# Batch 0's first tile on its own, the other tiles of its batch a slot or more behind, and two tiles of batch 2 turned by DMA

## The chip, the core and the metric

The kernel runs on one NeuronCore of a Trainium2 chip, as one program. The metric is the device time of one execution in microseconds. The core's engines are named as the profile names them: PE (TensorE, matmuls and transposes), PEld (its weight loads), DVE (VectorE), ACT (ScalarE), POOL (GpSimd) and SP (SyncE, which here only issues DMAs).

## The reference, cut to what matters

```python
# q, k, v: (8 batches, 8 heads, 576 rows, 64); all float32
kv  = einsum('bhsd,bhse->bhde', k, v)              # 64 x 64 for each head
out = einsum('bhsd,bhde->bhse', q, kv)
out = out / sqrt(mean(out*out, -1) + 1e-6) * g_norm
x   = out.transpose(0, 2, 1, 3).reshape(8, 576, 512)
xn  = (x - mean(x)) / sqrt(var(x) + 1e-6) * g_ln   # over the 512
y   = x + relu(xn @ w_ch1) @ w_ch2                 # 512 -> 2048 -> 512
```

A linear attention without a softmax, a normalisation within each head, and a feed-forward block with a layer norm and a residual.

## The kernel before

**Tiles.** A tile is 128 of a batch's rows. Each batch has four full tiles (0 to 3) and a remainder of 64 rows; the remainders of two batches form one tile of a last block called "rem". q, k and v are cast to bf16 by the loads, which POOL issues; matmuls take bf16 and add up in float32 in PSUM.

**From q to x.** For each batch, `kv_of` multiplies k and v and writes the result, two heads to a 128 x 128 block, into `kv_pack`. q is turned (rows to columns) so that it can be the stationary operand: by PE for batches 0 and 1 (`turn_first`, `turn_q`), by one DMA transpose issued by SP for the others (`turn_q_dma`). A tile then goes through the steps of class `Tile`: `o` (four matmuls on PE, into `o_ps`), `sq` (ACT squares it), `red` (DVE sums the squares of each head), `root` (ACT), the reciprocal (DVE, in `inv`), `y`, `x` and `xc` (DVE: divide; times g_norm with the row's sum beside it; minus the mean, times g_ln, in bf16), `var` (ACT, the variance) and `turn`, which brings xc's columns to the partitions as `xT_blk`: by four PE transposes and an ACT copy, or by one DMA transpose issued by SP. The factor 1/sqrt(var) is left out of the first matmul and applied at the very end, in `finish`.

**The two layers.** `mm1` multiplies quarters or less of w1 with xT and ACT writes the Relu into `m1`; `mm2_part` multiplies m1 with w2 into `p2`; `finish` (DVE) scales, adds x, and SP stores the result.

**Order.** The program is recorded as written (no scheduler): each engine runs its own instructions in the order in which the code emits them. `mm1` and `mm2_part` call `tick()`, which counts slots: a slot is one group of matmuls, some 0.9 us of PE work. Before each slot's matmuls `tick()` emits what `at(slot, fn)` has put there: that is how the tiles of later batches are woven into the matmuls of earlier ones. `plan_tile(s, make, turn_at, on_pe)` puts `o`, `sq`, `red` at slot s, `y`, `x`, `xc` at s+2, `var` at s+6, and `turn` at `turn_at`. Batch 0's first layer has slots 0 to 15, its second 16 to 31; batch 1 has 32 to 47 and 48 to 63; batch 2 has 64 to 79 (two tiles at a time) and 80 to 95. From batch 3 on, four tiles go together.

PSUM tiles come from pools that fix how many are in flight: `ps_m` (1), `ps_out` (2), `ps1` (3, `mm1`'s results among them) and `ps2` (2).

**The start.** Batch 0 has its own code. k comes in on SP's and ACT's queues in float32 and is cast by DVE and ACT; POOL issues v in two halves of two head pairs each, then q of rows 0 to 319 (`lo`) in two halves of four heads, w1's first quarter, the rest of q (`up`), the rest of w1, half of w2, batch 1, and the rest of w2. PE runs `fill` matmuls (on zeros, results unused) until data arrive. `kv_first` works by halves of the heads, and so do tiles 0 and 1, side by side: `half_turn` turns both tiles' q, `half_o` multiplies and squares, `half_red` reduces. For these two tiles x comes by a second matmul with kv times g_norm (`kv_g`; `o_g`, `x_g`), so that `y` is not needed. `halves_xc` and `halves_turn` make xT in two halves. The other tiles of batch 0 have their places in the agenda:

```python
at(1, lambda: turn_first(2, ps_m, "misc", nc.vector.tensor_copy))
at(1.1, lambda: halves_turn(1, xc1, ps_out, "ops"))
at(1.2, o2)     # o and sq of tile 2
at(1.3, x2)     # red, y, x, xc of tile 2
at(4, lambda: turn_first(3, ps_m, "misc"))
at(5, lambda: t[3].o())
at(5.1, x3)     # sq, red, y, x, xc of tile 3
at(6, lambda: t[2].turn(True))
at(9, lambda: turn_first(J, ps_m, "misc"))
at(10, lambda: t[3].turn(True))
```

Lines that the prediction names: L126, L127 and L129 load v and q; L196 is a fill; L266 is `sq`, L287 `red`, L297 `root`, L311 `x`, L321 `xc`; L337 and L339 are `turn`'s PE transposes and its ACT copy, L341 its DMA transpose; L402 is `mm1`'s matmul and L405 its Relu; L418 is `mm2_part`'s matmul; L183 is `turn_groups`, L541 `halves_turn`, L260 `o`.

Of the kernel before, what the change touches and what calls it, by code (L numbers as in the profile page):

```python
# [14 lines left out]
def kernel(  # L15
# [70 lines left out]
    def lo(t, b, h0=0, h1=H):  # L86
        return t[b, h0:h1, :S_LO, :].rearrange("h (p j) d -> p h j d", j=JJ)
# [35 lines left out]
    nc.vector.memset(fill_sb, 0.0)  # L123
    nc.sync.dma_start(k_f[:, :HP // 2], pairs(k, 0, HP // 2))
    nc.scalar.dma_start(k_f[:, HP // 2:], pairs(k, HP // 2, HP))
    nc.gpsimd.dma_start(v_p[:, :HP // 2], pairs(v, 0, HP // 2))  # L126
    nc.gpsimd.dma_start(v_p[:, HP // 2:], pairs(v, HP // 2, HP))  # L127
    for h0 in (0, H // 2):
        nc.gpsimd.dma_start(q_in[0][:64, h0:h0 + H // 2], lo(q, 0, h0, h0 + H // 2))  # L129
    load_w1(0)  # L130
    make_identity(nc, identity)
    nc.gpsimd.dma_start(q_in[0][64:, :, :J], up(q, 0))
# [44 lines left out]
    def turn_groups(tp, i, h0, h1):  # L177
        groups = ((0, 2 * i), (0, 2 * i + 1)) if i < 2 else ((64, 2 * i - 4), (64, 2 * i - 3))
        if i == J:
            groups = ((0, J),)  # L180
        for h in range(h0, h1):
            for half, (p0, j) in enumerate(groups):
                nc.tensor.transpose(  # L183
                    tp[h % 2 * D:h % 2 * D + D, (h - h0) // 2, half * 64:half * 64 + 64],
                    q_in[0][p0:p0 + 64, h, j, :], identity[p0:p0 + 64, p0:p0 + 64])
        return 64 * len(groups)
# [3 lines left out]
        n = turn_groups(tp, i, 0, H)  # L190
        copy(qts[0][:, i, :, :n], tp[:, :, :n])  # L191

    def fill(n, pool=ps2, tag="p2"):
        for _ in range(n):
            p1 = pool.tile([128, 512], f32, tag=tag, name="p1")
            nc.tensor.matmul(p1, lhsT=fill_sb[:, :128], rhs=fill_sb, start=True, stop=True)  # L196
            del p1

    def turn_q_dma(b):
        q_p = kv_in.tile([128, JJ, H, D], bf16, tag="qp", bufs=2)  # L200
# [6 lines left out]
    def kv_first():  # L207
        kvp = held[0] = kv_pack[0]
        g = g_norm_sb.to_broadcast([128, HP // 2, D])
        for i, (pe, te, po, to) in enumerate(((ps_m, "misc", ps1, "p1"), (ps1, "p1", ps1, "p1"))):  # L210
            even = pe.tile([128, HP // 2, D], f32, tag=te, name="even")
            odd = po.tile([128, HP // 2, D], f32, tag=to, name="odd")
            hps = slice(i * HP // 2, (i + 1) * HP // 2)
            for hp in range(hps.start, hps.stop):
                for j in range(JP):
                    js = slice(j * D, (j + 1) * D)
                    for hh, dst in ((0, even), (1, odd)):
                        rows = slice(hh * D, hh * D + D)
                        nc.tensor.matmul(dst[rows, hp - hps.start, :], lhsT=k_p[rows, hp, js],
                                         rhs=v_p[rows, hp, js],  # L220
                                         start=(j == 0), stop=(j == JP - 1))
            nc.vector.tensor_copy(kvp[:D, hps, :D], even[:D])
            nc.scalar.copy(kvp[D:, hps, D:], odd[D:])
            nc.vector.tensor_mul(kv_g[:D, hps, :D], even[:D], g[:D])
            nc.vector.tensor_mul(kv_g[D:, hps, D:], odd[D:], g[D:])
            del even, odd

    def kv_of(b):
        kv_ps = ps_m.tile([128, HP, D], f32, tag="misc", name="kv_ps")
# [228 lines left out]
    def at(slot, fn):  # L458
        agenda.setdefault(int(slot), []).append((slot, fn))
# [12 lines left out]
    del gl_row  # L472

    qts[0] = qt_pool.tile([128, JJ, HP, 128], bf16, tag="qt", name="qt")
    fill(18)
    kv_first()


    t = [main_tile(0, i, ps2, "p2") for i in range(4)]
    for i in range(2):  # L480
        t[i].ss = work.tile([128, H, 1], f32, tag="ss", bufs=4, name="ss")
    sqs = [work.tile([128, H, D], f32, tag="sq", name="sq") for _ in range(2)]
    banks = (((ps_out, "ops"), (ps_m, "misc")), ((ps_out, "ops"), (ps1, "p1")))
    copies = ((nc.scalar.copy, nc.scalar.copy), (nc.vector.tensor_copy, nc.vector.tensor_copy))

    def half_turn(half):
        hp0 = half * HP // 2
        tps = [ps2.tile([128, HP // 2, 128], bf16, tag="p2", name="tp") for _ in range(2)]
        for i in range(2):
            turn_groups(tps[i], i, 2 * hp0, 2 * hp0 + H // 2)  # L490
        for i in range(2):
            copies[half][i](qts[0][:, i, hp0:hp0 + HP // 2], tps[i])

    def half_o(i, half):
        hp0 = half * HP // 2
        pool, tag = banks[half][i]
        o = pool.tile([128, H // 2, D], f32, tag=tag, name="o_half")
        flat = o.rearrange("p h e -> p (h e)")
        for k2 in range(HP // 2):
            nc.tensor.matmul(flat[:, k2 * 128:(k2 + 1) * 128], lhsT=qts[0][:, i, hp0 + k2, :],  # L500
                             rhs=kv_pack[0][:, hp0 + k2, :], start=True, stop=True)
        nc.scalar.activation(sqs[i][:, half * H // 2:(half + 1) * H // 2], o, func=AF.Square)

    def half_red(i, half):
        hs = slice(half * H // 2, (half + 1) * H // 2)
        nc.vector.tensor_reduce(t[i].ss[:, hs], sqs[i][:, hs], axis=AX.X, op=ALU.add)

    half_turn(0)
    fill(2, ps_out, "ops")
    half_o(0, 0)  # L510
    half_turn(1)
    half_o(1, 0)
    half_o(0, 1)
    half_red(0, 0)
    half_red(0, 1)
    half_o(1, 1)
    t[0].root()
    half_red(1, 0)
    half_red(1, 1)
    t[0].o_g(ps1, "p1")  # L520
    t[1].o_g(ps1, "p1")
    fill(8)
    t[0].x_g()
    t[1].root()


    def halves_xc(i):
        x_blk, st, _ = t[i].blk
        for c in range(2):
            cs = slice(c * Dm // 2, (c + 1) * Dm // 2)  # L530
            xc = work.tile([128, Dm // 2], bf16, tag="xch", bufs=4, name="xc")
            nc.vector.scalar_tensor_tensor(xc, in0=x_blk[:, i, cs], scalar=st[:, 1, i:i + 1],
                                           in1=g_ln_sb[:, cs], op0=ALU.add, op1=ALU.mult)
            yield xc

    def halves_turn(i, xcs, pool, tag):
        xT = t[i].blk[2]
        for c, xc in enumerate(xcs):
            tp = pool.tile([128, 2, 128], bf16, tag=tag, name="tp")
            for kk in range(2):  # L540
                nc.tensor.transpose(tp[:, kk, :], xc[:, kk * 128:(kk + 1) * 128], identity)  # L541
            nc.scalar.copy(xT[:, 2 * c:2 * c + 2, i * 128:(i + 1) * 128], tp)

    halves_turn(0, halves_xc(0), ps_out, "ops")
    t[1].x_g()
    xc1 = list(halves_xc(1))


    def x2():
        t[2].red()  # L550
        t[2].y()
        t[2].x()
        t[2].xc()

    def x3():
        t[3].sq()
        t[3].red()
        t[3].y()
        t[3].x()
        t[3].xc()  # L560

    def o2():
        t[2].o()
        t[2].sq()
# [119 lines left out]
```

## Time and profile before

| | |
|---|---|
| Time, median of 5 runs | 292.21 us (292.13 to 292.37) |
| The profiled execution's own time | 292.21 us |
| Its span in the profile | 290.4 us |
| Granted TensorE clock | 1.00 |
| PE busy | 281.5 us, 97% of the span |
| ACT, DVE, POOL busy | 155.6, 150.9, 41.1 us |
| Chain that ended last | 84% PE |

Times within the profile count from the span's start. In an order of time, a line gives the start, the duration, the engine, the line of the code, the operation, what it writes and reads, how many such instructions are merged, and in square brackets how long the engine had been idle before and what ended that. A matmul's duration is the time until its result is there; the next one may start earlier, so the starts tell the pace: sixteen matmuls of 128 columns (one slot of the first layer) take 0.893 us from start to start.

### The profile page before, as it was taken

What the parts mean: (1) busy time and instruction counts of PE and PEld (TensorE: products, weight loads), DVE (VectorE), ACT (ScalarE), POOL (GpSimd) and SP (SyncE); (2) the same over time, 40 slices, a digit from 0 to 9 for tenths busy, and PEclk for the clock granted to TensorE, in tenths of its full rate; (3) what the DMA queues carried; (4) which work ended last, traced back from release to release, by engine and by line L of the source; (5) the groups of instructions that cost most, each with busy time, mean ns of one, the idle gap of its engine ahead of it and who ended that gap; (6) DMA issues with size and microseconds to landing.
All of it is one profiled execution on the core that took longest, in us unless ns stands there. A gap on an engine that the chain in (4) does not pass through costs nothing.

```text
span 290.4 us, 5777 instructions
## 1 busy us (share of the span) xinstructions
PE 281.5 (97%) x2294; PEld 159.5 (55%) x2320; DVE 150.9 (52%) x335; ACT 155.6 (54%) x341; POOL 41.1 (14%) x68
## 2 busy tenths in 40 slices
PE   8889999999999999999999999999999999999995
PEld 3579755995578744444444544444444444444444
DVE  5775028936996793666366935752578300220022
ACT  3467755885569931892189408930894066016500
POOL 8522520032050003200410023000000000000000
PEclk9999999999999999999999999999999999999999
DMA  7999999469789818994997279959202510131033
GB/s 213 203 206 205 201 202 219 103 102 191 145 147 193 109 42 150 213 168 88 151 202 107 50 145 198 167 78 168 54 18 53 112 36 0 38 81 27 2 72 72
DMA packets 63290, 35.84 MB, mean 123 GB/s; under 512 B 30748, under 2 KB 58268, under 8 KB 63264
## 3 DMA queue, kind: packets, MB, share of 16 engines
q0 software_dynamic: 28016, 17.76, 44.0%
q1 hardware_dynamic: 34736, 16.99, 30.0%
q10 hardware_dynamic: 512, 0.72, 0.8%
q8 instruction: 18, 0.29, 0.4%
q14 instruction: 8, 0.07, 0.1%
HBM read 36.71 MB, written 9.44 MB: 159 GB/s over the span
## 4 chain that ended last, share of the span: by engine, by line
PE 84%; DVE 5%; DMA 4%; ACT 2%; issue 2%; POOL 0%; SPq 0%; DVEq 0%; POOLq 0%
PE p L402 40%; PE p L418 38%; DMA v_in<-in_v_dram 2%; PE o_ps L260 2%; DMA out_dram<-o_sb 2%; PE kv_ps L235 2%; DVE o_sb L423 1%; DVE ss L287 1%; ACT m L405 1%; DVE x_blk L311 1%; DVE y L292 1%; PE tp L183 1%; DVE xc L321 1%; PE p L196 1%; ACT sq L266 0%
## 5 line engine op out<-in xcount | busy, mean ns | idle before, releaser
L402 PE MATMUL p<-xT_blk,w_sb 128*128 128x128 bf16 (+2 forms) x1017 | 131.7, 285 | 0.9 <-ACT m L405 0.3
L418 PE MATMUL p<-w_sb,m 128*128 128x512 bf16 (+2 forms) x590 | 126.9, 368 | 1.6 <-issue 0.8
L405 ACT ACTIVATE m<-p 128x512 bf16<-128x512 f32 x144 | 85.2, 597 | 41.7 <-PE p L402 39.7
L402 PEld LDWEIGHTS <-w_sb 128*128 128x128 bf16 x1024 | 78.4, 98 | 44.6 <-issue 1.1
L418 PEld LDWEIGHTS <-m 128*128 128x128 bf16 x608 | 56.8, 98 | 61.2
L423 DVE SCALAR_TENSOR_TENSOR o_sb<-p,rstd,x_blk 128x512 f32<-128x512 f32 (+2 forms) x38 | 27.4, 721 | 54.0 <-PE p L418 51.2
L266 ACT ACTIVATE sq<-o_ps 128x512 f32<-128x512 f32 x34 | 20.2, 595 | 41.2 <-PE o_ps L260 41.1
L329 ACT ACTIVATE dev<-x_blk,st_blk 128x512 f32<-128x512 f32 x36 | 25.7, 716 | 4.5 <-DVE st_blk L315 4.4
L287 DVE TENSOR_REDUCE ss<-sq 128x8 f32<-128x512 f32 x34 | 23.1, 679 | 8.4 <-ACT sq L266 8.4
L321 DVE SCALAR_TENSOR_TENSOR xc<-x_blk,st_blk,g_ln_sb 128x512 bf16<-128x512 f32 x34 | 25.6, 752 | 1.2
L292 DVE TENSOR_TENSOR y<-o_ps,inv 128x512 f32<-128x512 f32 x34 | 23.5, 692 | 2.8
L311 DVE SCALAR_TENSOR_TENSOR x_blk<-y,g_norm_sb 128x512 f32<-128x512 f32 x34 | 23.5, 692 | 1.2
L411 DVE RECIPROCAL rstd<-rstd 128x4 f32<-128x4 f32 x9 | 1.6, 175 | 39.3 <-ACT rstd L410 39.3
L304 DVE RECIPROCAL inv<-rms 128x8 f32<-128x8 f32 x36 | 7.2, 201 | 23.1 <-ACT rms L297 23.1
L98 POOL COPY gate<-qt 1x1 bf16<-1x1 bf16 x5 | 0.9, 178 | 114.8 <-DMA qt<-q_p 114.8
L297 ACT ACTIVATE rms<-ss,eps_sb 128x8 f32<-128x8 f32 x36 | 10.7, 298 | 9.8 <-DVE ss L287 9.1
L260 PEld LDWEIGHTS <-qt 128*128 128x128 bf16 (+1 forms) x152 | 10.0, 100 | 7.4 <-issue 1.7
L260 PE MATMUL o_ps<-kv_pack,qt 128*128 128x128 bf16 (+1 forms) x152 | 13.3, 220 | 0.2 <-DVE qt L191 0.2
L196 PE MATMUL p<-fill_sb 128*128 128x512 bf16 x27 | 9.2, 507 | 1.4 <-DVE eps_sb L137 1.2
L339 ACT COPY xT_blk<-tp 128x512 bf16<-128x512 bf16 x10 | 5.8, 580 | 2.3 <-PE tp L337 2.3
L329 ACT ACTIVATION_READ_ACCUMULATOR dev<-x_blk,st_blk 128x1 f32 x36 | 6.9, 191 | 0.0
L196 PEld LDWEIGHTS <-fill_sb 128*128 128x128 bf16 x28 | 3.2, 123 | 6.0 <-issue 3.8
(79 smaller groups left out, 118.3 us busy)
## 6 DMA issues: line engine op xcount, KB each, us to landing
out_dram<-o_sb SPq DMA_DIRECT2D x70, 128.0 KB, 2.4
w_sb<-in_moe_w_ch_dram POOLq DMA_DIRECT2D x8, 512.0 KB, 13.9
k_in<-in_k_dram POOLq DMA_DIRECT2D x7, 320.0 KB, 5.5
v_in<-in_v_dram POOLq DMA_DIRECT2D x7, 320.0 KB, 8.6
q_in<-in_q_dram POOLq DMA_DIRECT2D x7, 320.0 KB, 12.6
q_in<-in_q_dram POOLq DMA_DIRECT2D x8, 256.0 KB, 12.7
k_in<-in_k_dram POOLq DMA_DIRECT2D x7, 256.0 KB, 6.5
v_in<-in_v_dram POOLq DMA_DIRECT2D x7, 256.0 KB, 10.2
```

The source lines that it names most:

```text
L196: nc.tensor.matmul(p1, lhsT=fill_sb[:, :128], rhs=fill_sb, start=True, stop=True)
L260: nc.tensor.matmul(flat[rows, hp * 128:(hp + 1) * 128], lhsT=lhsT_of(hp), rhs=kvp[:, hp, :], start=True, stop=True)
L266: nc.scalar.activation(self.sq_t, self.o_ps, func=AF.Square)
L287: nc.vector.tensor_reduce(self.ss, self.sq_t, axis=AX.X, op=ALU.add)
L292: nc.vector.tensor_mul(self.y_t, self.o_ps, self.inv().to_broadcast([128, H, D]))
L311: nc.vector.scalar_tensor_tensor(x_blk[:, ts].rearrange("p (h d) -> p h d", h=H), in0=self.y_t, scalar=1.0, in1=g_norm_sb.to_broadcast([12 ...
L321: nc.vector.scalar_tensor_tensor(self.xc_t, in0=x_blk[:, self.ts], scalar=st[:, 1, self.ts:self.ts + 1], in1=g_ln_sb, op0=ALU.add, op1=ALU ...
L329: nc.scalar.activation(dev, x_blk[:, ts], func=AF.Square, bias=st[:, 1, ts:ts + 1], accum_out=st[:, 2, ts:ts + 1])
L402: nc.tensor.matmul(p1[:, i, :], lhsT=w1_sb[:, kk, de * 128:(de + 1) * 128], rhs=blk[2][:, kk, sl], start=(kk == 0), stop=(kk == nK - 1))
L405: nc.scalar.activation(m1[:, de0:de0 + per, sl], p1, func=AF.Relu)
L418: nc.tensor.matmul(p2[:, c0:c1], lhsT=m1s[b][:, de, ts * 128:(ts + 1) * 128], rhs=w2_sb[:, de, c0:c1], start=(de == 0), stop=(de == nDe - 1))
L423: nc.vector.scalar_tensor_tensor(o_sb[:, c0:c1], in0=p2[:, c0:c1], scalar=rstds[b][:, ts:ts + 1], in1=blks[b][0][:, ts, c0:c1], op0=ALU.mu ...
```

## The change

- v is loaded as three head pairs, then one; q's rows of tile 0 alone come between the two, and the rest of q's first 320 rows behind them. The number of loads is the same.
- `kv_first` becomes the class `KvFirst`, used for three head pairs and then for one, with its matmuls, copies and products with g_norm as separate steps.
- Tile 0 goes alone through the start. Tile 1's q is turned behind it, its reduction and root stand behind tile 0's xc.
- Slot 1 holds the q turns of tile 2, the remainder and tile 3 (all copied by ACT), tile 2's steps and tile 1's xT; slot 3 holds tile 3's steps (`before_1`, `before_3`).
- The first layer of batch 0 goes in other pieces, with three quarters of tile 2 before the last quarter of tiles 0 and 1; its second layer goes in a half, a quarter and a quarter.
- Fills: 18, 2, 3 and 2, where there were 18, 2 and 8; fills of one call share a PSUM tile.
- Batch 2's tiles start at slots 44, 48, 53 and 58 (before 46, 51, 55 and 59); its tiles 0 and 1 are turned by DMA at slots 50 and 54 instead of by PE at 53 and 58, tiles 2 and 3 by PE at 61 and 67 (before 63 and 68).

```diff
-    nc.gpsimd.dma_start(v_p[:, :HP // 2], pairs(v, 0, HP // 2))
-    nc.gpsimd.dma_start(v_p[:, HP // 2:], pairs(v, HP // 2, HP))
-    for h0 in (0, H // 2):
-        nc.gpsimd.dma_start(q_in[0][:64, h0:h0 + H // 2], lo(q, 0, h0, h0 + H // 2))
+    nc.gpsimd.dma_start(v_p[:, :HP - 1], pairs(v, 0, HP - 1))
+    nc.gpsimd.dma_start(q_in[0][:64, :, :2], lo(q, 0)[:, :, :2])
+    nc.gpsimd.dma_start(v_p[:, HP - 1:], pairs(v, HP - 1, HP))
+    nc.gpsimd.dma_start(q_in[0][:64, :, 2:], lo(q, 0)[:, :, 2:])
...
-    fill(18)
-    kv_first()
-    t = [main_tile(0, i, ps2, "p2") for i in range(4)]
...
+    fill(18)
+    kv_a = KvFirst(0, HP - 1, ((ps_m, "misc"), (ps1, "p1")))
+    kv_b = KvFirst(HP - 1, HP, ((ps1, "p1"), (ps1, "p1")))
+    t = [main_tile(0, 0)] + [main_tile(0, i, *((ps1, "p1") if i == 1 else (ps2, "p2")))
+                             for i in range(1, 4)]
...
+    kv_a.mms()
+    kv_a.copies()
+    turn_first(0, ps2, "p2")
+    kv_a.times_g()
+    fill(2)
+    kv_b.mms()
+    kv_b.copies()
+    part_o(kv_a)
+    part_o(kv_b)
+    part_sq(kv_a)
+    part_sq(kv_b)
+    kv_b.times_g()
+    t[0].o_g(ps2, "p2")
+    part_red(kv_a)
+    part_red(kv_b)
     t[0].root()
-    half_red(1, 0)
-    half_red(1, 1)
-    t[0].o_g(ps1, "p1")
+    turn_first(1, ps_m, "misc")
+    dead = fill(3)
+    t[1].o()
+    t[1].sq()
     t[1].o_g(ps1, "p1")
-    fill(8)
+    fill(2, dead)
+    del dead
     t[0].x_g()
-    t[1].root()
...
     halves_turn(0, halves_xc(0), ps_out, "ops")
+    t[1].red()
+    t[1].root()
     t[1].x_g()
     xc1 = list(halves_xc(1))
...
+    def before_1():
+        turn_first(2, ps_m, "misc")
+        turn_first(J, ps2, "p2")
+        t[2].o()
+        halves_turn(1, xc1, ps_out, "ops")
+        t[2].sq()
+        turn_first(3, ps_m, "misc")
+        x_of(2)
+
+    def x_of(i):
+        t[i].red()
+        t[i].y()
+        t[i].x()
+        t[i].xc()
+
+    def before_3():
+        t[3].o()
+        t[3].sq()
+        x_of(3)
...
-    at(1, lambda: turn_first(2, ps_m, "misc", nc.vector.tensor_copy))
-    at(1.1, lambda: halves_turn(1, xc1, ps_out, "ops"))
-    at(1.2, o2)
-    at(1.3, x2)
-    at(4, lambda: turn_first(3, ps_m, "misc"))
-    at(5, lambda: t[3].o())
-    at(5.1, x3)
+    at(1, before_1)
+    at(3, before_3)
     at(6, lambda: t[2].turn(True))
-    at(9, lambda: turn_first(J, ps_m, "misc"))
...
-    for j, s, tn in ((0, 46, 53), (1, 51, 58), (2, 55, 63), (3, 59, 68)):
-        plan_tile(s, lambda j=j: main_tile(2, j), tn, True)
+    for j, s, tn in ((0, 44, 50), (1, 48, 54), (2, 53, 61), (3, 58, 67)):
+        plan_tile(s, lambda j=j: main_tile(2, j), tn, j > 1)
...
-    for ts, c0, c1 in ((0, 0, 8), (1, 0, 8), (0, 8, 12), (1, 8, 12), (0, 12, 16), (1, 12, 16),
-                       (2, 0, 16), (3, 0, 16)):
+    for ts, c0, c1 in ((0, 0, 4), (1, 0, 4), (0, 4, 8), (1, 4, 8), (0, 8, 12), (1, 8, 12),
+                       (2, 0, 12), (0, 12, 16), (1, 12, 16), (2, 12, 16), (3, 0, 16)):
         mm1(0, ts, 1, c0, c1)
...
-    for ts in range(4):
-        mm2_part(0, ts, p2s[ts], 0, nDe // 2)
+    for de0, de1 in ((0, nDe // 2), (nDe // 2, nDe * 3 // 4)):
+        for ts in range(4):
+            mm2_part(0, ts, p2s[ts], de0, de1)
     for ts in range(4):
         p2 = p2s[ts]
         p2s[ts] = None
-        mm2_part(0, ts, p2, nDe // 2, nDe)
+        mm2_part(0, ts, p2, nDe * 3 // 4, nDe)
         finish(0, ts, p2)
```

`KvFirst` does what `kv_first` did for one half of the heads, with a slice of head pairs of any size; `part_o`, `part_sq` and `part_red` are `half_o` and `half_red` for such a slice of tile 0.

More of the change, by code (lines that the diff above doesn't have):

```diff
@@ L191, in turn_first, with fill @@
         copy(qts[0][:, i, :, :n], tp[:, :, :n])
-    def fill(n, pool=ps2, tag="p2"):
+    def fill(n, p1=None):
+        if p1 is None:
+            p1 = ps2.tile([128, 512], f32, tag="p2", name="p1")
         for _ in range(n):
-            p1 = pool.tile([128, 512], f32, tag=tag, name="p1")
             nc.tensor.matmul(p1, lhsT=fill_sb[:, :128], rhs=fill_sb, start=True, stop=True)
-            del p1
+        return p1
     def turn_q_dma(b):
@@ L205, in turn_q_dma, with __init__, mms, copies @@
         qts[b] = q_t
[L207 to L214, printed above, removed]
+    class KvFirst:
+        def __init__(self, hp0, hp1, pools):
+            self.hps, self.pools = slice(hp0, hp1), pools
+        def mms(self):
+            n = self.hps.stop - self.hps.start
+            (pe, te), (po, to) = self.pools
+            self.even = pe.tile([128, n, D], f32, tag=te, name="even")
+            self.odd = po.tile([128, n, D], f32, tag=to, name="odd")
+            for hp in range(self.hps.start, self.hps.stop):
                 for j in range(JP):
                     js = slice(j * D, (j + 1) * D)
-                    for hh, dst in ((0, even), (1, odd)):
+                    for hh, dst in ((0, self.even), (1, self.odd)):
                         rows = slice(hh * D, hh * D + D)
-                        nc.tensor.matmul(dst[rows, hp - hps.start, :], lhsT=k_p[rows, hp, js],
-                                         rhs=v_p[rows, hp, js],
+                        nc.tensor.matmul(dst[rows, hp - self.hps.start, :],
+                                         lhsT=k_p[rows, hp, js], rhs=v_p[rows, hp, js],
                                          start=(j == 0), stop=(j == JP - 1))
[L222 to L226, printed above, removed]
+        def copies(self):
+            nc.vector.tensor_copy(kv_pack[0][:D, self.hps, :D], self.even[:D])
+            nc.scalar.copy(kv_pack[0][D:, self.hps, D:], self.odd[D:])
+        def times_g(self):
+            g = g_norm_sb.to_broadcast([128, self.hps.stop - self.hps.start, D])
+            nc.vector.tensor_mul(kv_g[:D, self.hps, :D], self.even[:D], g[:D])
+            nc.vector.tensor_mul(kv_g[D:, self.hps, D:], self.odd[D:], g[D:])
+            del self.even, self.odd
     def kv_of(b):
@@ L474 @@
     qts[0] = qt_pool.tile([128, JJ, HP, 128], bf16, tag="qt", name="qt")
+    held[0] = kv_pack[0]
     fill(18)
-    kv_first()
-    t = [main_tile(0, i, ps2, "p2") for i in range(4)]
[L480 to L516, printed above, removed]
+    kv_a = KvFirst(0, HP - 1, ((ps_m, "misc"), (ps1, "p1")))
+    kv_b = KvFirst(HP - 1, HP, ((ps1, "p1"), (ps1, "p1")))
+    t = [main_tile(0, 0)] + [main_tile(0, i, *((ps1, "p1") if i == 1 else (ps2, "p2")))
+                             for i in range(1, 4)]
@@ new lines, with part_o @@
+    t[0].ss = work.tile([128, H, 1], f32, tag="ss", bufs=4, name="ss")
+    sq_0 = work.tile([128, H, D], f32, tag="sq", name="sq")
+    o_0 = {}
+    def part_o(kv_x):
+        hp0, hp1 = kv_x.hps.start, kv_x.hps.stop
+        o_0[hp0] = ps_out.tile([128, 2 * (hp1 - hp0), D], f32, tag="ops", name="o_part")
+        flat = o_0[hp0].rearrange("p h e -> p (h e)")
+        for hp in range(hp0, hp1):
+            nc.tensor.matmul(flat[:, (hp - hp0) * 128:(hp - hp0 + 1) * 128],
+                             lhsT=qts[0][:, 0, hp, :], rhs=kv_pack[0][:, hp, :],
+                             start=True, stop=True)
@@ new lines, in part_sq, with part_red @@
+    def part_sq(kv_x):
+        hp0, hp1 = kv_x.hps.start, kv_x.hps.stop
+        nc.scalar.activation(sq_0[:, 2 * hp0:2 * hp1], o_0.pop(hp0), func=AF.Square)
+    def part_red(kv_x):
+        hs = slice(2 * kv_x.hps.start, 2 * kv_x.hps.stop)
+        nc.vector.tensor_reduce(t[0].ss[:, hs], sq_0[:, hs], axis=AX.X, op=ALU.add)
+    kv_a.mms()
[8 more added lines that the diff above has]
+    part_sq(kv_a)
@@ L544 @@
     halves_turn(0, halves_xc(0), ps_out, "ops")
+    t[1].red()
+    t[1].root()
     t[1].x_g()
     xc1 = list(halves_xc(1))
[L549 to L555, printed above, removed]
-        t[3].sq()
[L557 to L564, printed above, removed]
+    def before_1():
[13 more added lines that the diff above has]
+        t[3].o()
+        t[3].sq()
+        x_of(3)
     def next_loads():
```

## The prediction

> **What bounds the kernel now.** I read the page first, then TensorE's order of time, then ScalarE and VectorE around the place where TensorE fills up, then the late waits and the landings of the first loads.
>
> ```profile
> PE 281.5 (97%) x2294; PEld 159.5 (55%) x2320; DVE 150.9 (52%) x335; ACT 155.6 (54%) x341; POOL 41.1 (14%) x68
> ```
>
> TensorE (PE) is the bound over the span. Its order of time shows from where:
>
> ```profile
> 15.04 0.68 PE L541 MATMUL tp<-identity,xc 128*128 128x128 bf16 x4 [0.84 <-DVE xc L532]
> 15.78 1.34 PE L402 MATMUL p<-xT_blk,w_sb 128*128 128x128 bf16 x16
> 17.05 0.44 PE L183 MATMUL tp<-identity,q_in 64*64 64x64 bf16 x16
> 17.42 0.40 PE L541 MATMUL tp<-identity,xc 128*128 128x128 bf16 x4
> 18.02 0.40 PE L260 MATMUL o_ps<-kv_pack,qt 128*128 128x128 bf16 x4 [0.20 <-DVE qt L191]
> ...
> 33.37 4.48 PE L418 MATMUL p<-w_sb,m 128*128 128x512 bf16 x19
> ```
>
> The first real matmul (slot 0) starts at 15.78, the second layer (slot 16) at 33.37. From 18.02 on PE has only cracks. So the time moves with the start of slot 16, with PE work after it, and with the few waits left. The nearest thing to a wait is on ScalarE, whose queue runs in order (all engines' order of time):
>
> ```profile
> 18.45 0.60 ACT L266 ACTIVATE sq<-o_ps 128x512 f32<-128x512 f32 x1
> 19.09 0.69 DVE L287 TENSOR_REDUCE ss<-sq 128x8 f32<-128x512 f32 x1 [1.12 <-ACT sq L266]
> 19.81 0.30 ACT L297 ACTIVATE rms<-ss,eps_sb 128x8 f32<-128x8 f32 x1 [0.75 <-DVE ss L287]
> ...
> 22.10 0.75 DVE L321 SCALAR_TENSOR_TENSOR xc<-x_blk,st_blk,g_ln_sb 128x512 bf16<-128x512 f32 x1
> ...
> 23.62 0.69 DVE L287 TENSOR_REDUCE ss<-sq 128x8 f32<-128x512 f32 x1 [0.77 <-ACT sq L266]
> ...
> 24.34 0.30 ACT L297 ACTIVATE rms<-ss,eps_sb 128x8 f32<-128x8 f32 x1 [0.75 <-DVE ss L287]
> ...
> 24.55 0.58 ACT L405 ACTIVATE m<-p 128x512 bf16<-128x512 f32 x1
> ...
> 25.03 0.58 ACT L339 COPY xT_blk<-tp 128x512 bf16<-128x512 bf16 x1
> ```
>
> ACT stands 0.75 us at each root (L297) for VectorE's reduction, and the Relus and the xT copy behind it stand too. Before, this is covered: the copy at 25.03 serves slot 8, which PE reaches at 25.66 anyway. The same thing shows late, where it does cost:
>
> ```profile
> 90.36 0.82 PE L402 MATMUL p<-xT_blk,w_sb 128*128 128x256 bf16 x6 [0.30 <-ACT m L405]
> ```
>
> PE had stood there since 89.92 (89.03 plus eight matmuls of 0.112), 0.44 us in issue, for a Relu queued behind the root of batch 3's first tile (root at 87.85 after 0.85 us idle, for a reduction that VectorE reached late).
>
> **The first loads.** Issue plus time to landing gives 7.48 for v's first half (1.26 + 6.2), 8.96 for its second, 9.76 and 10.66 for q's halves. 256 rows of v (1152 B) thus take 1.48 us, a pair of heads 0.74; 512 rows of q (640 B) take 1.70. The new q loads have 256-B and 384-B rows. No load of before has these; its packet records have 60, 69, 98 and 107 ns for rows of 512, 640, 1024 and 1152 B, on a line of about 20 ns + 0.075 per byte, which gives 39 and 49. So q's first part takes 1.70 x 39/69 = 0.96, its rest 1.21; the other end is the price of 640-B rows, 1.70 each. I take the line, since four sizes lie on it. Landings: three pairs of v 8.22, q of tile 0 9.18, last pair 9.92, rest of q 11.1, w1's first quarter 13.6 (before 13.16, needed at 14.8). Everything behind on the POOL queue slips by 0.47; w1's second quarter (before 17.80) is wanted at 19.3, the third (20.33) at 21.3, the last (23.00) at slot 9: covered, but only just if rows cost 1.70 (then 1.7 us of slip).
> [...]
>
> **The walk to slot 0.** Durations are the rows' own. PE's 18 fills end at 8.08, the 54 kv matmuls (0.016 each, +0.19) run 8.27 to 9.31, the transposes of tile 0 9.14 to 9.58, two fills to 9.83, the last pair's 18 matmuls 9.95 to 10.43. Its copies end at 10.66, its o matmul at 10.9; the squares (0.49, then 0.27 for a quarter) end at 11.32, the reductions at 11.93, the root starts at 11.97 where it started at 12.73. From there the steps are those of before (root to reciprocal 0.34, no longer held by tile 1's reductions; to x 0.31; to the second xc half 1.30; its copy): slot 0 starts at 14.82 with its first half and 15.21 with its second, and ends its issue at 15.99 (before 17.05). Gain so far about 1 us.
>
> **Why it does not last.** In the changed order tile 1's reduction stands behind tile 0's xc on VectorE: 14.30; its root 15.07, x 15.71, second xc half 17.02 to 17.52 (before 17.40). Slot 1's prefix now holds the transposes of tiles 2, 3 and the remainder (0.37, 0.37, 0.24) and tile 1's, so slot 1's matmuls start at 18.3 and 18.55, with PE idle about 0.65 for tile 2's copy, which moved from VectorE to ACT behind a Relu. ACT does tile 1's two xT copies to 18.41, then tile 2's square: 18.41, as before's 18.45. From there by the rows above: reduction 19.05, root 19.77, xc of tile 2 at 22.07.
> Now the step that decides. Tile 3's square is emitted two slots earlier, at slot 3, and its root stands on ACT ahead of the Relus of slots 3, 4, 5 and of tile 2's xT copy. Its reduction must wait for VectorE to finish tile 2: 22.07 + 0.67 = 22.74. Root 0.72 later, 23.46; Relus 23.67, 24.15, 24.63; copy 25.11; PE may go on 0.63 later, 25.74. And slot 6 is now tile 2 itself. PE ends slot 5 at 23.1 and tile 2's transposes at 23.4: it stands 2.3 us.
> At 25.66 before stands at slot 8, at 25.74 after at slot 6 with the remainder's transposes done: 0.08 + 2 x 0.893 - 0.24 = +1.6 us at slot 16. Its bounds: +1.4 if each step is 0.05 faster, +2.3 if q's rows cost 1.70 each.
>
> **Later.** Taking the second layer of batch 0 in quarters keeps the matmul count, and w2's last quarter (landed 42.54, used at 43.35 before) is wanted three groups later: nothing. Its four stores bunch, and VectorE, in one stretch of work from 44.41 to 57.30, has the same work in it from the first store on less what it did before it: batch 2's q copy ends at 57.3 again (before's frame, shifted like PE), q^T lands at 62.3, and slot 44, which now wants it, starts at 62.86; before it was slot 46, at 64.65. Cover 0.5 us; if it goes, PE stands for the excess.
> Two tiles of batch 2 turn by DMA: eight transposes leave PE, 2 x 0.223 = -0.45, and two copies of 0.58 leave ACT. SP gets two issues of 1.2 us ahead of stores and of batch 3's q^T; it is idle from 60.5 to 71.7 before. They land in 2.4 to 9.0 us (median 3.6, L341); issued by 74, wanted at slot 64, 82.7: covered. Both tiles start two or three slots earlier, in VectorE's idle 60.5 to 65.7. So VectorE reaches batch 3's first reduction about 0.65 sooner against PE (2.5 us after its o instead of 3.15), the root no longer holds the Relu of 90.36: -0.45 (bounds -0.45 and 0). Fewer fills (25 for 28) cost and bring nothing before slot 0.
> Sum: 292.21 (the profiled execution's own time, span 290.4 and 1.8 outside; the same as the median) + 1.6 - 0.45 - 0.45 = 292.9 us; its own range 292.4 to 293.4.
>
> **Rivals.** (1) Faster: ACT is not held at tile 3's root, because the chain to it runs more than 1.3 us ahead of my walk. Then the copy follows slot 5's Relu, 23.73 + 0.58, slot 6 starts at 24.35, slot 16 at +0.2, the time is 291.5. It decides from a copy that ends before 24.4. For it: the start is 1 us earlier; against: every step is a row. (2) Small rows are dear: 1.70 each adds 0.75 to the chain, 293.6. (3) PE's clock. The fills from 1.20 to 7.12 start about 0.43 apart and later ones 0.21: PE starts at half speed. The stall of 0.84 before 15.04 did not bring that back; one of 2.3 is not in the trace. If it does, up to 5.9 us at half speed, +1.5 to +2.9: 294.4 to 295.8.
> [...]
> (4) The change does nothing: the stall is half of mine, and the two -0.45 pay for it, 292.2. (5) q^T of batch 2 lands after slot 44: +0.5, 293.4.
>
> **Chances.** About 0.2% (0.58 us) is what a measurement of this kernel can tell from no change. Forecast 0.58, of which 0.18 lies within 292.79; (1) 0.13; (2) 0.10; (3) 0.04; (4) 0.08; (5) 0.07. Faster 0.13; same 0.18 + 0.08 = 0.26; slower 0.40 + 0.10 + 0.04 + 0.07 = 0.61. The range leaves out (1) and (3): 292.0 to 294.0.
>
> **What would show it.** Slot 0 near 14.8; PE idle over 2 us before the matmuls of slot 6, released by an xT copy; ACT idle at a root near 23.5 for VectorE's reduction; slot 16 at about 35.0; no gap before the matmuls of batch 2's second half. A copy ending by 24.4, or slot 16 at or before 33.7, makes it wrong; so does a wait on q^T at slot 44.

## The result, and the profile after

| | before | after |
|---|---|---|
| Time, median of the runs | 292.18 us (47 runs) | 293.39 us (26 runs) |
| Ratio | | 1.0051, interval 1.0039 to 1.0064 |
| First matmul of slot 0, us in the profile | 15.78 | 15.04 |
| Slot 16 (second layer of batch 0) | 33.37 | 36.73 |
| From slot 16 to PE's last matmul | 253.28 | 252.54 |
| Profiled execution's own time, span, granted clock | 292.21, 290.4, 1.00 | 294.74, 292.9, 0.994 |

The change makes the kernel slower by half a per cent. The executions of the changed kernel fall in two groups, and the median lies at the border: of 27, 14 took 293.0 to 293.4 us and 13 took 294.5 us or more. The profiled one is of the second group; what divides them is part of the result.

TensorE's order of time around the start (window 14.5 to 40; columns as above). Line numbers of the changed kernel are higher than before: its `o` is L270, `sq` L276, `red` L297, `root` L307, `xc` L331, `turn`'s transposes and copy L347 and L349, `mm1` and its Relu L412 and L415, `mm2_part` L428.

```profile
15.04 1.34 PE L412 MATMUL p<-xT_blk,w_sb 128*128 128x128 bf16 x16
...
17.54 0.40 PE L270 MATMUL o_ps<-kv_pack,qt 128*128 128x128 bf16 x4 [0.76 <-ACT qt L191]
...
25.95 5.36 PE L412 MATMUL p<-xT_blk,w_sb 128*128 128x128 bf16 x64 [2.21 <-ACT xT_blk L349]
...
36.73 3.62 PE L428 MATMUL p<-w_sb,m 128*128 128x512 bf16 x15
```

Slot 0 is 0.74 us earlier than before. Then PE stands 0.76 us for tile 2's q copy, and 2.21 us ahead of slot 6 for tile 2's xT. Why xT is late is read from ScalarE and VectorE (all engines' order of time, same place):

```profile
21.15 0.60 ACT L276 ACTIVATE sq<-o_ps 128x512 f32<-128x512 f32 x1
...
22.28 0.75 DVE L331 SCALAR_TENSOR_TENSOR xc<-x_blk,st_blk,g_ln_sb 128x512 bf16<-128x512 f32 x1
22.95 0.68 DVE L297 TENSOR_REDUCE ss<-sq 128x8 f32<-128x512 f32 x1
...
23.66 0.30 ACT L307 ACTIVATE rms<-ss,eps_sb 128x8 f32<-128x8 f32 x1 [1.91 <-DVE ss L297]
23.87 1.55 ACT L415 ACTIVATE m<-p 128x512 bf16<-128x512 f32 x3
...
25.30 0.60 ACT L349 COPY xT_blk<-tp 128x512 bf16<-128x512 bf16 x1
```

After tile 3's square ACT stands 1.91 us at tile 3's root, because VectorE reduces tile 3 only after tile 2's xc. Three Relus that were ready have to wait behind the root, and the copy that slot 6 wants is behind them.

There is a second loss. The four groups of the first layer from 25.95 on last 5.20 us to the transposes at 31.15, where four slots of 0.893 are 3.57. The windows of one microsecond show why (start and end, length, busy time and number of instructions of PE, PEld, DVE, ACT and POOL, then the granted clock, and last the DMA engines' share and GB/s):

```profile
26.00:27.00 1.00, 1.00 (x17) 1.00 (x17) 0.71 (x1) 0.00 (x0) 0.76 (x1) 0.84 1.24 201
27.00:28.00 1.00, 1.00 (x12) 1.00 (x11) 0.00 (x0) 0.60 (x1) 0.00 (x0) 0.50 1.34 201
...
30.00:31.00 1.00, 1.00 (x20) 1.00 (x19) 0.00 (x0) 0.55 (x1) 0.87 (x2) 0.96 1.38 201
```

PE's clock is halved from 26.68 to 30.09 (granted 0.50), shortly behind the stall. In those 3.41 us PE does the work of 1.7 us (12 matmuls in the microsecond from 27.00, 22 in that from 31.00), so slot 16 comes 1.64 us later than it would. The executions at 294.5 and above have a mean clock of 0.988 to 0.994; those at 293.0 to 293.4 one of 0.998 to 1.000, but for two of 0.992; these two were not profiled.

Later on PE gains. In batch 2's first layer nothing stands where before had its stall at 90.36 (TensorE's order of time, window 60 to 96):

```profile
92.14 4.09 PE L412 MATMUL p<-xT_blk,w_sb 128*128 128x256 bf16 x36
```

### The profile page after: what moved, and what is told of

Same layout as the page of the kernel before. It is cut to its first block, busy times and chain, and to the rows that moved or that the text cites. A ratio compares the mean times of both kernels' runs of the same rounds, so it can differ in the third digit from the quotient of the medians.

```text
span 292.9 us, 5752 instructions
## 1 busy us (share of the span) xinstructions
PE 281.5 (96%) x2282; PEld 159.9 (55%) x2309; DVE 150.1 (51%) x331; ACT 155.6 (53%) x339; POOL 40.9 (14%) x68
## 4 chain that ended last, share of the span: by engine, by line
PE 91%; DMA 2%; DVE 2%; ACT 2%; issue 1%; DVEq 0%; POOLq 0%
PE p L412 43%; PE p L428 42%; PE o_ps L270 3%; DMA v_in<-in_v_dram 2%; PE kv_ps L245 2%; ACT m L415 1%; PE tp L347 1%; PE tp L170 0%; DVE xc L545 0%; PE odd L224 0%; DVE ss L512 0%; DVE xc L331 0%; DVE x_blk L288 0%; PE even L224 0%; DVE x_blk L321 0%
## 5 line engine op out<-in xcount | busy, mean ns | idle before, releaser
L412 PE MATMUL p<-xT_blk,w_sb 128*128 128x128 bf16 (+2 forms) x1017 | 132.7, 288 | 2.8 <-ACT xT_blk L349 2.2
L428 PE MATMUL p<-w_sb,m 128*128 128x512 bf16 (+2 forms) x590 | 126.8, 368 | 1.6 <-issue 0.9
L415 ACT ACTIVATE m<-p 128x512 bf16<-128x512 f32 x144 | 85.3, 596 | 45.7 <-PE p L412 43.5
L412 PEld LDWEIGHTS <-w_sb 128*128 128x128 bf16 x1024 | 80.1, 99 | 46.3 <-issue 2.8
L428 PEld LDWEIGHTS <-m 128*128 128x128 bf16 x608 | 56.8, 98 | 61.7
L276 ACT ACTIVATE sq<-o_ps 128x512 f32<-128x512 f32 x35 | 20.8, 595 | 42.4 <-PE o_ps L270 42.4
L297 DVE TENSOR_REDUCE ss<-sq 128x8 f32<-128x512 f32 x35 | 23.7, 678 | 10.4 <-ACT sq L276 10.4
L331 DVE SCALAR_TENSOR_TENSOR xc<-x_blk,st_blk,g_ln_sb 128x512 bf16<-128x512 f32 x34 | 25.6, 752 | 1.2
L307 ACT ACTIVATE rms<-ss,eps_sb 128x8 f32<-128x8 f32 x36 | 10.7, 297 | 9.5 <-DVE ss L297 8.7
L270 PEld LDWEIGHTS <-qt 128*128 128x128 bf16 (+1 forms) x156 | 10.1, 100 | 8.6 <-issue 1.7
L270 PE MATMUL o_ps<-kv_pack,qt 128*128 128x128 bf16 (+1 forms) x156 | 13.7, 220 | 1.0 <-ACT qt L191 1.0
L197 PE MATMUL p<-fill_sb 128*128 128x512 bf16 x23 | 8.1, 508 | 1.3 <-DVE eps_sb L137 1.2
L245 PEld LDWEIGHTS <-k_in 128*64 128x64 bf16 x280 | 5.0, 112 | 2.7 <-issue 2.6
L248 ACT CAST kv_pack<-kv_ps 64x256 bf16<-64x256 f32 x7 | 2.6, 367 | 7.3 <-PE kv_ps L245 7.1
```

The lines of the kernel that those rows point to most:

```text
L245: nc.tensor.matmul(kv_ps[hh * D:hh * D + D, hp, :], lhsT=k_in[b % NB][:, h, j, :], rhs=v_in[b % NB][:, h, j, :], start=(j == 0), stop=(j = ...
L270: nc.tensor.matmul(flat[rows, hp * 128:(hp + 1) * 128], lhsT=lhsT_of(hp), rhs=kvp[:, hp, :], start=True, stop=True)
L276: nc.scalar.activation(self.sq_t, self.o_ps, func=AF.Square)
L297: nc.vector.tensor_reduce(self.ss, self.sq_t, axis=AX.X, op=ALU.add)
L331: nc.vector.scalar_tensor_tensor(self.xc_t, in0=x_blk[:, self.ts], scalar=st[:, 1, self.ts:self.ts + 1], in1=g_ln_sb, op0=ALU.add, op1=ALU ...
L412: nc.tensor.matmul(p1[:, i, :], lhsT=w1_sb[:, kk, de * 128:(de + 1) * 128], rhs=blk[2][:, kk, sl], start=(kk == 0), stop=(kk == nK - 1))
```

## The experiments

Every kernel was timed against the kernel before on the same chip, in five rounds. "Slot 16" and "rest" (slot 16 to PE's last matmul) are from the one profiled execution of each, so slots 0 and 16 carry that execution's load times (e5's profiled one started late); the time is the median.

| kernel | slot 0 | stall before slot 6 | slot 16 | rest | time, us | ratio to before |
|---|---|---|---|---|---|---|
| e1 tile 3's root behind the copy | 15.17 | 0.94 | 33.97 | 252.52 | 292.00 | 1.0000 (0.9987 to 1.0012) |
| e2 tiles 0, 1 before tile 2 | 15.13 | 0.75 | 33.74 | 252.57 | 291.74 | 0.9983 (0.9974 to 0.9992) |
| e3 both | 14.88 | none | 33.06 | 252.53 | 291.37 | 0.9976 (0.9964 to 0.9989) |
| e4 nine fills in the stall | 15.03 | 0.26 | 35.09 | 252.54 | 293.07 | 1.0030 (1.0019 to 1.0042) |
| e5 before + batch 2's plan | 16.40 | none | 33.99 | 252.56 | 291.78 | 0.9978 (0.9967 to 0.9989) |
| e6 e4, batch 2's plan put back | 14.99 | none | 35.92 | 253.43 | 294.00 | 1.0060 (1.0047 to 1.0074) |
| e7 e3, tile 3 turned at slot 11 | 14.99 | none | 32.90 | 252.58 | 290.86 | 0.9947 (0.9935 to 0.9959) |
| e8 e7, second layer in halves | 14.94 | none | 32.85 | 252.55 | 291.00 | 0.9958 (0.9943 to 0.9973) |
| e9 e7, tile 1's xT before tile 2 | 14.93 | none | 34.22 | 252.57 | 292.34 | 1.0013 (0.9994 to 1.0031) |
| e10 three fills in the stall | 15.56 | 1.55 | 35.63 | 252.54 | 293.05 | 1.0028 (1.0019 to 1.0038) |
| e11 e7, q by heads behind v | 17.13 | none | 34.91 | 252.54 | 292.85 | 1.0029 (1.0013 to 1.0046) |

The theory was that the early start is lost at one place, ACT's queue at tile 3's root, and that the halved clock is a consequence of the stall. The rivals were that the order of the matmuls (tile 2 wanted at slot 6) is the cause by itself, and that the two groups of times have another origin.

**e1: tile 3's reduction and root behind the copy.**

```diff
     def before_3():
         t[3].o()
         t[3].sq()
-        x_of(3)
...
     at(6, lambda: t[2].turn(True))
+    at(6.1, lambda: x_of(3))
```

> The changed kernel with tile 3's reduction, root and the rest emitted behind tile 2's xT copy in slot 6, instead of in slot 3. Theory (ScalarE's queue: tile 3's root holds the Relus of slots 3 to 5 and tile 2's copy): the Relus run as PE delivers, the copy ends near 24.6 instead of 25.9, slot 6 starts 1.3 us earlier, the time is about 291.8 us, and PE's clock stays at 1.00 because the stall is 1.0 us instead of 2.2. Rival (the stall comes from the late start of tiles 1 and 2, or from w1's last quarter): slot 6 stays within 0.3 us of 25.95 and the time at 293.0 or above.

TensorE's order of time in e1, the first line behind the stall:

```profile
24.81 3.73 PE L412 MATMUL p<-xT_blk,w_sb 128*128 128x128 bf16 x64 [0.94 <-ACT xT_blk L349]
```

Slot 6 starts at 24.81 where it started at 25.95; the clock is 1.00 over the profiled execution, but two of the eleven executions (293.02 and 293.08) had a mean of 0.994 and 0.993, where 1.00 was expected of all. The stall is not gone: the copy at 24.18 still stands behind slot 5's Relu, and PE has nothing but tile 2 to do. The median of 292.00 is 1.07 under that of e4, which has the stall at the full clock, and 0.2 above the 291.8 expected. The theory's mechanism holds: at the full clock slot 16 was 1.72 us later than before (e4), and moving the root takes away 1.12 of it (33.97 against 35.09).

**e2: the order of the first layer as before.** The last quarter of tiles 0 and 1 stands ahead of tile 2 again.

```diff
-                       (2, 0, 12), (0, 12, 16), (1, 12, 16), (2, 12, 16), (3, 0, 16)):
+                       (0, 12, 16), (1, 12, 16), (2, 0, 16), (3, 0, 16)):
```

> The changed kernel with the last quarter of tiles 0 and 1 in slots 6 and 7 and all of tile 2 from slot 8, as before the change; tile 3's root left where it is. Theory: PE no longer needs the copy at slot 6, but needs the PSUM tile of slot 3, whose Relu stands behind tile 3's root until 24.5: the stall shrinks from 2.2 to 0.9 us, the time is about 291.7 us. If the order of the pieces alone were the cause, the stall would go altogether: 290.7 us. If w1's last quarter were late (landed at 23.2), slot 6 would wait for it: 293 us.

TensorE's order of time in e2, the same place:

```profile
24.59 3.73 PE L412 MATMUL p<-xT_blk,w_sb 128*128 128x128 bf16 x64 [0.75 <-ACT m L415]
```

Slot 6 now wants no new xT, and it waits all the same: for a Relu that is queued behind the root and has not emptied its PSUM tile. So the root on ACT costs whatever slot 6 is, and 1.5 us less of it reaches PE when tile 2 is not due. 291.74 as expected.

**e3: both.** The two diffs above together.

> Both edits: tile 3's root behind tile 2's copy, and tiles 0 and 1 in slots 6 and 7. Theory: no stall at slot 6, slot 16 about 2.3 us earlier than in the changed kernel at full clock, 290.7 us, 1.4 us faster than before the change. Rival (something else ends the wait at slot 6, or later stages give it back): 291.5 us or more.

TensorE's order of time in e3, tile 3's transposes:

```profile
27.47 0.40 PE L347 MATMUL tp<-identity,xc 128*128 128x128 bf16 x4 [0.31 <-DVE xc L331]
```

No stall is left at slot 6. Tile 3, now later, is 0.31 us late at its own transposes in slot 10; the time of 291.37 is above the 290.7 expected by this and by the spread of its six runs (291.03 to 292.31).

**e4: nine fills in the stall.** The order of the changed kernel is kept; PE multiplies zeros while it would stand.

```diff
     at(6, lambda: t[2].turn(True))
+    at(6.1, lambda: fill(9))
```

> The changed kernel with nine more fills (1.9 us of PE) behind tile 2's transposes, in the stall itself; the stall ends as before. [...] Rival (the slower executions have another cause than an idle PE): the two groups near 293.2 and 294.6 stay.

TensorE's order of time in e4, slot 6 and slot 16:

```profile
25.94 3.73 PE L412 MATMUL p<-xT_blk,w_sb 128*128 128x128 bf16 x64 [0.26 <-ACT xT_blk L349]
...
35.09 4.48 PE L428 MATMUL p<-w_sb,m 128*128 128x512 bf16 x19
```

All seven executions took 293.01 to 293.26 us at a clock of 0.998 or more, one group near the 293.1 that I had expected. Slot 6 starts as late as in the changed kernel (25.94), the second group has gone, slot 16 is at 35.09. So the 1.64 us between 35.09 and 36.73 are the clock's, and with the fills in the stall it fell in none of the seven.

**e5: batch 2's plan alone, on the kernel before.**

```diff
-    for j, s, tn in ((0, 46, 53), (1, 51, 58), (2, 55, 63), (3, 59, 68)):
-        plan_tile(s, lambda j=j: main_tile(2, j), tn, True)
+    for j, s, tn in ((0, 44, 50), (1, 48, 54), (2, 53, 61), (3, 58, 67)):
+        plan_tile(s, lambda j=j: main_tile(2, j), tn, j > 1)
```

> The kernel before with nothing of the change but batch 2's plan: its tiles start at slots 44, 48, 53 and 58, its tiles 0 and 1 are turned by DMA at 50 and 54. Theory (two terms of the prediction, each -0.45): eight transposes leave TensorE for certain, 0.45 us; the stall of 0.44 us ahead of batch 2's second half goes too. 291.3 with both, 291.75 with the first alone; slot 16 stays at 33.4. Rival: batch 2's transposed q, a slot and a half earlier in want of a transfer that starts no earlier here, comes late for slot 44 and the time stays at 292.2 or rises; then a gap stands before the first o matmul of batch 2.

The rest is 252.56 where before has 253.28, and the stretch behind PE's last matmul is 3.65 where it was 3.79: 0.86 us together, and 0.90 was expected. PE goes through the place of the old stall (its order of time in e5):

```profile
89.42 4.53 PE L402 MATMUL p<-xT_blk,w_sb 128*128 128x256 bf16 x40
```

The median gained only 0.49 against 292.27 in the same rounds. The difference is not in the span: most of e5's spans are 289.5 to 289.7 against 290.3 to 290.4, but their times lie 2.10 to 2.19 us above the span in all twelve, where all other kernels, before among them, have 1.7 to 1.9. Some 0.36 us was added outside what the profile shows. What adds it is open.

**e6: the same plan taken out of e4.** The diff is that of e5, reversed.

> The changed kernel with nine fills in the stall before slot 6 (293.07 by itself, one group of times) and with batch 2's plan put back as it was before the change. Theory: the later part of the change is worth what it was seen to be worth from slot 16 to the last matmul, 0.74 us, so 293.8; 293.5 if the transposes alone count, 294.0 if both terms hold in full. Rival: the gain behind slot 16 comes from elsewhere (the quarters of batch 0's second layer, the order of the stores): 293.1.

TensorE's order of time in e6, batch 2's first layer:

```profile
91.58 1.04 PE L412 MATMUL p<-xT_blk,w_sb 128*128 128x256 bf16 x8
92.90 3.36 PE L412 MATMUL p<-xT_blk,w_sb 128*128 128x256 bf16 x29 [0.28 <-ACT m L415]
```

The old stall is back in the new kernel: eight matmuls of 0.112 from 91.58 end their issue at 92.48, the next starts at 92.90. 294.00 is 0.93 more than e4, near the 0.90 of both terms in full (294.0 in the expectation); one of the six executions had a halved clock, and without it the difference is 0.88. The plan is worth what was forecast, and the rival (the quarters, the stores) is out. The profiled execution of e6 shows more, told below under the clock.

**e7: e3 with tile 3's transposes one slot later.**

```diff
-    at(10, lambda: t[3].turn(True))
+    at(11, lambda: t[3].turn(True))
```

> The run with both repairs (291.37: tile 3's reduction and root behind tile 2's xT copy, tiles 0 and 1 before tile 2) with tile 3's transposes at slot 11 in place of 10, where a gap of 0.31 us stood before them. Theory: the gap goes, slot 16 0.3 us earlier (32.75), 290.8 to 291.1. Rival: the copy of tile 3 then becomes late for slot 12, and the gap returns there: 291.4.

TensorE's order of time in e7, from behind tile 3's transposes to slot 16:

```profile
28.23 4.84 PE L412 MATMUL p<-xT_blk,w_sb 128*128 128x128 bf16 x80
32.90 3.40 PE L428 MATMUL p<-w_sb,m 128*128 128x512 bf16 x14
```

Between 17.49, where tile 2's q copy is waited for as in the changed kernel, and slot 16 PE has no idle stretch of 0.15 us. Slot 16 starts at 32.90, 0.47 ahead of before. 290.86 us is the best time of the study, 0.5% under before and 0.9% under the changed kernel (290.86 / 293.39).

**e8: batch 0's second layer in halves again.**

```diff
-    for de0, de1 in ((0, nDe // 2), (nDe // 2, nDe * 3 // 4)):
-        for ts in range(4):
-            mm2_part(0, ts, p2s[ts], de0, de1)
+    for ts in range(4):
+        mm2_part(0, ts, p2s[ts], 0, nDe // 2)
...
-        mm2_part(0, ts, p2, nDe * 3 // 4, nDe)
+        mm2_part(0, ts, p2, nDe // 2, nDe)
```

> The run before with batch 0's second layer in two halves again, as before the change. Theory (the prediction priced the quarters at nothing): the same time within 0.2 us. Rival: w2's last quarter lands late for a second layer that starts at 32.75 and asks for it three groups earlier (it landed at 42.7): a gap before the eighth group, 0.1 to 0.5 us more.

291.00 (290.87 to 291.11, one at 292.01) against 290.86 (290.73 to 291.05), the rest 252.55 against 252.58: the same. The quarters cost and bring nothing that shows here.

**e9: tile 1's xT ahead of tile 2's steps**, an attempt to take away the 0.76 us in slot 1.

```diff
     def before_1():
         turn_first(2, ps_m, "misc")
-        turn_first(J, ps2, "p2")
-        t[2].o()
         halves_turn(1, xc1, ps_out, "ops")
+
+    def before_2():
+        turn_first(J, ps2, "p2")
+        t[2].o()
         t[2].sq()
         turn_first(3, ps_m, "misc")
         x_of(2)
...
+    at(2, before_2)
```

> The best run so far (both repairs, tile 3's transposes at slot 11, 290.86) with tile 1's xT transposes ahead of tile 2's o in slot 1, and the remainder's q, tile 2's o and square and tile 3's q moved to slot 2. There TensorE stood 0.76 us for tile 2's q copy, and slot 1 started at 18.46 though tile 1's xc was done at 17.7. Theory: slot 1 starts near 17.7, slot 16 by 0.5 to 0.7 earlier (32.2 to 32.4), 290.2 to 290.4. Rival: the wait for the q copy moves to slot 2 with the transposes and nothing is won: 290.9.

TensorE's order of time in e9, tile 1's transposes, slots 1 and 2, tile 2's transposes:

```profile
17.29 0.68 PE L554 MATMUL tp<-identity,xc 128*128 128x128 bf16 x4 [0.65 <-DVE xc L545]
18.04 1.34 PE L412 MATMUL p<-xT_blk,w_sb 128*128 128x128 bf16 x16
...
20.25 1.07 PE L412 MATMUL p<-xT_blk,w_sb 128*128 128x128 bf16 x16
...
24.62 0.40 PE L347 MATMUL tp<-identity,xc 128*128 128x128 bf16 x4 [0.24 <-DVE xc L331]
```

A miss for the theory and for its rival: 292.34, 1.48 us worse than e7. Slot 1 starts at 18.04, 0.42 earlier than e7's 18.46, but PE now waits there with nothing in hand, first 0.65 for xc, then for the second half's copy; tile 2's `o` and the q transposes that filled those waits in e7 come as 0.95 us of work of their own between slot 1 and slot 2 (19.30 to 20.25). Tile 2's `o` comes at 19.55 instead of 17.49, and PE waits for its xc before 24.62.

**e10: three fills in the stall.**

```diff
     at(6, lambda: t[2].turn(True))
+    at(6.1, lambda: fill(3))
```

> The changed kernel with three fills, 0.64 us, in the 2.2-us stall before slot 6; 1.6 us of it stay idle. Theory, from the clock records of all runs so far: the clock is halved where TensorE streams columns in under some 0.42 of a 3.41-us window (0.30 and 0.41 in the two windows after which it fell, 0.44 and more in all others). Three fills lift the poorest window from 0.30 to 0.49, so there is one group of times at 293.0 to 293.3 as with nine fills. Rival: the idle time in a window decides, as little as 1.23 us of it in one run that was halved: then about three executions in four would still be halved and lie at 294.5 to 294.7.

TensorE's order of time in e10, the fills and slot 6:

```profile
24.11 0.81 PE L197 MATMUL p<-fill_sb 128*128 128x512 bf16 x3
26.47 3.73 PE L412 MATMUL p<-xT_blk,w_sb 128*128 128x128 bf16 x64 [1.55 <-ACT xT_blk L349]
```

Nine executions, all at a clock of 0.999 or more: seven of 292.88 to 293.17, and two of 293.63 and 293.70. The profiled one is that of 293.63, and its first loads came late (PE's first products of k and v start at 8.58 and the transposes of tile 0's q at 9.71, against 8.36 and 9.19 in the changed kernel). A stall of 1.55 us did not halve the clock in this execution (1.00 in the profile). So three fills do what nine did, and the idle time alone does not decide.

**e11: q by heads, behind all of v.**

```diff
-    nc.gpsimd.dma_start(q_in[0][:64, :, :2], lo(q, 0)[:, :, :2])
     nc.gpsimd.dma_start(v_p[:, HP - 1:], pairs(v, HP - 1, HP))
-    nc.gpsimd.dma_start(q_in[0][:64, :, 2:], lo(q, 0)[:, :, 2:])
+    for h0 in (0, H // 2):
+        nc.gpsimd.dma_start(q_in[0][:64, h0:h0 + H // 2], lo(q, 0, h0, h0 + H // 2))
```

> The run of 290.86 with the loads of the start in the order v (three head pairs), v (the last), q of the first 320 rows in two halves of four heads (rows of 640 B), as q was loaded before the change. Theory: q of tile 0 is whole only at about 10.7 in place of 9.0, its transposes follow the last pair's products in place of lying ahead of them, the root of tile 0 and all behind it come 0.7 to 1.0 us later, 291.6 to 291.9. Rival: the wait for tile 0's q is hidden by the chain through the last pair: 290.9 to 291.1.

TensorE's order of time in e11, the second half of the transposes of tile 0's q:

```profile
10.66 0.32 PE L183 MATMUL tp<-identity,q_in 64*64 64x64 bf16 x8 [0.50 <-DMA q_in<-in_q_dram]
```

q of tile 0 is whole at 10.61 (9.0 in e7), and the last pair's products start at 11.44 (9.99 in e9, which loads as e7 does): 1.45 later, because the program has them behind the transposes and the two fills. The two executions at the full clock took 292.29 and 292.30, 1.44 above e7, where 0.7 to 1.0 was expected; I had left out that a late q holds the last pair's products too. The other ten had a clock of 0.994 or less and took 292.57 to 294.49: 0.3 to 2.2 us more, at the lower clock. At the full clock, loading tile 0's q by its rows and ahead of the last pair of v is thus worth 1.4 us in this program; the run changes the cut of q and its place together.

## Why the prediction was right, and what it mis-sized

The forecast was 292.9 with a range of 292.0 to 294.0, and slower at 0.61; the median is 293.39. The mechanism is the one forecast: ACT is held at tile 3's root, PE stands 2.2 us for it, and 0.86 of the forecast 0.90 us is won back later. That the median lies inside the range has luck in it: of the 26 executions it is taken over, 14 were in the faster group, and with two of these in the slower one it would have been 294.5.

**The loads.** The line through the four packet sizes held for the small rows: in the changed kernel's packet records, rows of 256 and 384 B take 41 and 51 ns (the line has 39 and 49). The loads took somewhat less than forecast: q of tile 0 0.82 us (9.14 after v's 8.32; forecast 0.96), the rest of q 1.05 (10.86 after 9.81; forecast 1.21), v's last pair 0.67 (forecast 0.74). Rival 2 (1.70 each) is out. Small rows cost more per byte here (0.160 ns at 256 B and 0.133 at 384 B, against 0.108 at 640 B), as the line has it; the packets of 512 B took 60 ns, on the same line.

**The start.** The root of tile 0 starts at 12.18 (forecast 11.97), slot 0 at 15.04 (14.82), 0.74 ahead of before instead of 1.0.

**The stall.** Tile 2's square 18.62 (18.41), its xc 22.28 (22.07), tile 3's reduction 22.95 (22.74), the root 23.66 (23.46), the copy 25.30 (25.11), slot 6 25.95 (25.74): the walk is right in every step and 0.2 late throughout, from the start's 0.2. PE stood 2.21 us (2.3). At the full clock slot 16 is at 35.09 (e4), 1.72 later than before, where the forecast had 1.6. Rival 1 (not held) is out.

**Later.** Both terms together: 0.74 between slot 16 and PE's last matmul and 0.12 behind it, 0.86 where 0.90 was forecast; e6 gives 0.93. q^T of batch 2 landed at 65.64 and its first `o` started at 66.22 without a wait, so rival 5 is out and its cover of 0.5 us was sized right. Put together, 292.21 + 1.72 - 0.86 = 293.07: e4's time is made up of these terms and no other.

**The clock.** The term that was mis-sized is rival 3. Its price was right (1.5 to 2.9; measured 1.64), its chance of 0.04 was not: going by times and mean clocks it came in 13 of 27 executions, and this puts the median at 293.39 instead of 293.1 (e4) or 293.2 (the median of the 14 others). Of the 0.49 us above the forecast, 0.12 is the stall's, 0.04 the later gain's, and the rest the clock's. No row of before shows what a stall of 2.3 us does to the clock, and the chance was my estimate alone, with the stall of 0.84 us as the one case without effect. It was too low: the stall was 2.21 us, and the clock fell behind it.

In the changed kernel's profile the granted clock changes at 6.20, 26.68, 30.09 and 292.92, which lie 6, 1 and 77 times 3.413 us apart; in before's it changes at 7.08 and 290.38, 83 times 3.413 apart. The 3.41 us ahead of the fall, from 23.27 to 26.68, have 2.21 us of idle time and 1.2 us of work in them.

What else counts than idle time is seen in stretches of 3.41 us in other runs. Halved behind the stretch: e6 from 14.06 to 17.47 with 1.23 us idle, and e11 from 9.65 to 13.06 with 0.86. Not halved: e10 from 23.76 to 27.17 with 1.55, and before from 13.90 to 17.32 with 1.14. The case of e6, where no stall of more than 0.76 us stands (windows of one microsecond, columns as above):

```profile
16.00:17.00 1.00, 0.73 (x30) 0.51 (x27) 0.93 (x4) 0.64 (x2) 0.63 (x1) 1.00 1.24 204
17.00:18.00 1.00, 0.51 (x6) 0.52 (x7) 0.68 (x2) 0.71 (x2) 0.00 (x0) 0.74 1.24 208
18.00:19.00 1.00, 1.00 (x21) 0.76 (x19) 0.00 (x0) 0.65 (x3) 0.68 (x1) 0.50 1.23 205
```

The clock falls at 17.47, behind a stretch that holds transposes of 64 columns, waits for copies and sixteen matmuls. I estimated each stretch's work from the matmuls in its rows: columns by 0.436 ns (0.893 us over the 2048 columns of a slot), by the part of 128x128 that the form has (a quarter for 64x64). By that the three halved stretches hold 0.31 (the changed kernel), 0.36 (e11) and 0.38 (e6) of their 3.41 us, those not halved 0.36 (before) and 0.50 (e10). The work done separates them better than the idle time, but not cleanly; I chose this measure after the runs, and none tested it. Columns alone, whatever the form, do not separate them: e11's halved stretch holds 0.64 by that count, that of before, not halved, 0.46. So the bound of 0.42 in e10's expectation does not hold, although no execution of e10 was halved, as forecast there; what decides is open. Why the halving came in about half of the changed kernel's executions is not shown, since one of them was profiled; before had 6 of 68 executions at 293.3 to 293.6 and a clock of 0.992 or 0.993, and none of these was profiled.

## What to carry to other kernels

When a step moves up in an engine's queue, ask what it waits for there: a root that waits 1.9 us for VectorE holds back every ready Relu and copy behind it, and the repair is to move the waiting instruction behind them, or to give PE other work than the one that the held copy feeds. A gain at the start pays only once the first consumer that runs dry has been moved too: the earlier start gained nothing at slot 16 until both repairs were made, and then 0.3 to 0.5 us. And a stall of 2.21 us on TensorE had a price of 1.64 us beyond its length here, by time and mean clock in 13 of 27 executions, and three cheap fills took it away.

## What the runs showed of the hardware that I had not expected

- TensorE's clock was halved for 3.41 us after a stall of 2.21 us, at a cost of 1.64 us: seen in the one profile of the changed kernel, and by time and mean clock in 12 more of 27 executions. With three or nine fills in that stall and nothing else changed (e10, e4) no execution of 16 had a mean clock under 0.998; e6, which has the nine fills too, was halved in one of six, at another place.
- It was halved also behind stretches of 3.41 us with only 1.23 us (e6) and 0.86 us (e11) of idle time, where the rest of the stretch was mostly transposes, small products and single groups.
- The time outside the span is 1.7 to 1.9 us in the runs of twelve kernels, and 2.10 to 2.19 in all twelve runs of e5, a kernel that differs from before only in batch 2's plan. No run explains it.
- Loads cast from float32 with rows of 256 and 384 B in SBUF took 0.82 and 1.05 us for 512 rows, 1.87 together, where the same bytes in rows of 640 B had taken 1.70: a tenth more. Packets of 256, 384, 512 and 640 B took 41, 51, 60 and 69 ns.
